# A list scheduler's table: sampled values asked for earlier, first keys and queries later, raw weights assumed later, first token load behind a weight block

## The chip, the cores and the metric

The kernel runs on one NeuronCore of a Trainium2 chip. The metric is the device time of one execution in microseconds (us); lower is better. TensorE (PE) multiplies matrices, VectorE (DVE) and ScalarE (ACT) work elementwise, GpSimd (POOL) does small copies and subtractions, and SyncE (SP) issues every DMA of this kernel. PSUM is the memory that PE writes to, SBUF the one that all engines share. A semaphore is how one engine, or a DMA that has landed, lets another go on.

## The reference

Block-sparse attention in float32, over 4 batches, 8 heads, 768 positions and 64 dimensions, feeds a two-layer MLP over the 3072 tokens.

```python
block, n_blocks, window = 32, 24, 1
mask = np.abs(blk_i - blk_j) <= window
mask = mask | (blk_i == 0) | (blk_j == 0) | (blk_i == n_blocks - 1) | (blk_j == n_blocks - 1)
for qb in range(n_blocks):
    for kb in sampled_blocks[qb]:                 # three sampled key blocks for each block of queries
        mask[qb * block:(qb + 1) * block, kb * block:(kb + 1) * block] = True
scores = np.where(mask, scale * (q @ k.T), -1e9)
attn = softmax(scores); attn_out = attn @ v
...
h = x @ w_in                                      # 512 -> 2048
r = np.maximum(h, 0.0)
out = (s * (r * r) + b) @ w_out                   # 2048 -> 512
```

## The kernel before, in words

**Attention.** The work is cut into 52 slots (`T["ORD"]`). Slots 0 to 25 are batches 0 and 1, slots 26 to 51 batches 2 and 3. A slot is either dense (kind "d": the rows that see all 768 keys, loads `qr..d` and `v` of 384 KB), sparse (kind "s": tile row t = 0 to 4, 352 key columns) or the last tile row (kind "h"). The first four slots are dense. For slot i, PE runs s(i), the scores (L694 and L708 with plain keys `kt`, L720 with sampled keys `kg`), t(i), the transposes of the exponentials (L771), a(i), the product with the values (L805 and L816 with plain values, L830 with the sampled values `vg`), and xT(i), a transpose of the result (L842). PE's line is fixed by hand as t(i), xT(i-1), s(i+2), a(i). DVE takes the row maxima (L735) and scales the result (L836), ACT does the exponentials (L747), both copy transposed tiles `pt` out of PSUM (L777, L775), ACT copies the result (L847, tile `xst`), and SP writes it to DRAM as `xd` (L859, the spill).

**Sampled values.** `gather_v` reads the sampled value blocks of one tile row for two batches in 12 DMAs of 128 KB (L637), each at an address that SP has loaded from `vidx` (L630), which DVE computes from the sampled block numbers (`sbi`). There are two `vg` buffers; `vg0` names tile row 0 of the first batches' pair.

**Weights.** `w_in` and `w_out` come as float64. `decode_f64` turns each of 32 blocks (`i0` to `i15`, `o0` to `o15`, order `T["WL"]`) into a high and a low float32 half in nine steps: L75, L77, L78, L83 (the high half), L84, L85 (the low half) on DVE, L79, L81, L82 on ACT. A raw block of 512 KB (L57, `raw_i5`, `raw_o14`) sits in one of three buffers `kraw`, which are shared with the two token loads `xraw0` (L348, 384 KB each: the `xd` of batch 0's first half read back). ACT and DVE split `xraw0` into the halves `x0` (L361 on ACT, L363 on DVE).

**MLP.** A sub is one group of 384 tokens by one of 16 blocks of 128 hidden columns f. mlp1 multiplies tokens by `w_in` (L389 to L391, three products for the halves), ACT takes the relu (L394), DVE the square (L398), ACT adds b and rounds (L402, L403), POOL subtracts for the low half (L407), and mlp2 multiplies by `w_out` (L424 to L426). The first 30 subs are ordered by the planner: subs 0 to 3 are f = 0 and 1 of groups 0 and 1, then f counts up with groups 0 and 1 in turn, so that subs 26 and 27 are f = 13, subs 28 and 29 f = 14. The rest is a fixed loop.

**The planner.** Class `Plan` is given every operation with its engine, an assumed cost, a priority number (in units: a slot has 2 or 4 units, N is their count) and what it depends on. In each step it takes, on the engine that can start first, the operation with the lowest number among those that can start then. What comes out is the program order of each engine, which the chip then follows in order. SP's DMAs use eight semaphores in rotation, so an issue waits until the DMA eight before it has landed. The numbers touched here:

```python
"LATE": 3000.0     # ns added to the assumed landing of a raw weight block
"GV": [7.0, ...]   # units ahead of first use at which the vg gathers of tile row t fall due
"KL": [46.0, ...]  # the same for the keys kt of batch b
"QL": 18.0         # the same for queries; slot 0 has 50 instead
```

The function that holds all of this, as the diff touches it:

Of the kernel before, what the change touches and what calls it, by code (L numbers as in the profile page):

```python
# [24 lines left out]
F32_MOST = float(0x7F7FF000)  # L25
T = {
# [6 lines left out]
}  # L33
# [65 lines left out]
class Plan:  # L99
# [15 lines left out]
    def op(self, eng, cost, prio, fn, deps=(), alloc=(), use=(), order=(), nbytes=0, cols=0, late=0.0):  # L115


        o = Plan.Op()
        o.cost, o.prio, o.fn, o.nbytes, o.cols, o.late = cost if isinstance(cost, dict) else {eng: cost}, prio, fn, nbytes, cols, late
        o.pick = isinstance(cost, dict)  # L120
        o.deps, o.order, o.alloc = [d for d in deps if d], [d for d in order if d], alloc
        o.end, o.seq = None, len(self.ops)
        for k in (*alloc, *use):
            self.users.setdefault(k, []).append(o)
        self.ops.append(o)
        return o
# [76 lines left out]
def kernel(  # L203
# [131 lines left out]
    def decode(which, f):  # L335
        tail = (lambda: scratch("kraw", 2 * NW, f"raw_{which}{f}").bitcast(I32), *parts())
        if which == "i":
            src, view = w_in[:, f * P:(f + 1) * P].rearrange("(c p) n -> p c n", p=P), win
        else:
            src, view = w_out[f * P:(f + 1) * P, :], wout  # L340
        return decode_f64(nc, NW, src, b_top, b_most, *tail, lambda: view(f, 0), lambda: view(f, 1))
# [101 lines left out]
    with ExitStack() as es:  # L443
# [35 lines left out]
        def load_q(key, par):  # L479
            kind, b, t = key  # L480
            if par == 0:
                qraw[key] = qp.tile([P, NPAIR, P], F32, tag="qr", name=f"qr{b}_{t}{kind}")
            rows = slice(par * D, (par + 1) * D)
            nc.sync.dma_start(out=qraw[key][rows], in_=q_dup[b, t, rows, par::2, :] if kind == "s" else q_edge[b, int(kind == "d"), rows, par::2, :])
# [380 lines left out]
        op = plan.op  # L865
# [39 lines left out]
        for b in range(B):  # L905
            need = min(first[("k", b, p)] for p in range(NPAIR))
            for p in range(NPAIR):
                prev_k = kld[(b, p)] = op("s", 450, need - T["KL"][b] + T["KS"] * p, lambda b=b, p=p: load_k(b, p),
                                          alloc=[] if p else [(f"kt{b}", b)], use=[(f"kt{b}", b)] if p else [], order=[prev_k], nbytes=557e3)
# [7 lines left out]
        for need, b, t in sorted((n, *k[1:]) for k, n in first.items() if k and k[0] == "g"):  # L917
# [3 lines left out]
            for m in range(nq * NSL):  # L921
                pk = op("g", 230 if m else 1100, need - T["GK"] + m * 0.5, lambda gk=gk, m=m: gk(m), [o_si, *(kld[(b, p)] for p in range(NPAIR))],
                        alloc=[("kg", key)] if m == 0 else [], use=[(f"kt{b}", b)] + ([("kg", key)] if m else []), order=[pk])
# [6 lines left out]
            for m in range(nq * NSL + (nq if t == NSP else 0)):  # L930
                pv = op("s", 510 if m else 1300, need - T["GV"][t] + m * 0.5, lambda gv=gv, m=m: gv(m), [o_si],
                        alloc=[("vg", key)] if m == 0 else [], use=[("vg", key)] if m else [], order=[pv], nbytes=131e3)
# [4 lines left out]
        pq = pvl = o_m = o_e = o_rc = o_ev = None  # L937
        spills, tensor, lqs = {}, {}, {}
# [3 lines left out]
        for i, (kind, b, t, x) in enumerate(slots):  # L942
            u, full, cost, col = unit_of[i], kind == "s", costs[kind], cols[kind]
            nu, ng, nk = (2, 2, 2) if kind == "d" else (4, 1, 2)
            qk = slots[i][:3]
            if qk not in lqs:
                for par in range(2):
                    pq = lqs[qk] = op("s", 450, u - (T["QL"] if i else 50) + 0.1 * par, lambda qk=qk, par=par: load_q(qk, par), alloc=[] if par else [("qr", qk)],
                                      use=[("qr", qk)] if par else [], order=[pq], nbytes=131e3)
            lq = lqs[qk]  # L950
            lv = {}
# [7 lines left out]
            for k in range(nk):  # L959
# [3 lines left out]
                       alloc=[("B", ("s", *y)) for y in keys], use=[("qr", qk), (f"kt{b}", b)])  # L963
# [10 lines left out]
            for j in range(nu):  # L974
                n, ms_ = u + j, []
                for g in range(ng):
                    o_m = op("v", {"s": 600, "d": 680, "h": 500}[kind], n + T["MP"], lambda n=n, g=g: maximum(n, g),
                             [*s_of[(n, g)], *([] if kind == "d" else [o_ss]), *ms_],
                             alloc=[("P", (n, g))] + ([("nm", n)] if g == 0 else []), use=[("B", ("s", n, g))] + ([("nm", n)] if g else []),
                             order=[o_m])  # L980
                    ms_.append(o_m)
                for g in range(ng):
                    top = g == 0 and j == 0
                    o_e = op("a", {"s": 780, "d": 800, "h": 700}[kind], n + T["EP"], lambda n=n, g=g: exp(n, g), ms_,
                             alloc=[("dn", i)] if top else [], use=[("P", (n, g)), ("nm", n)] + ([] if top else [("dn", i)]), order=[o_e])
# [9 lines left out]
            for j in range(nu):  # L995
                pr = j if kind == "d" else 0
                o = op("p", cost[3], u, lambda i=i, j=j: av_static(i, j), cols=col[3], deps=[*evs[j], lv[pr]],
                       alloc=[] if j else [("o", i)], use=[("v", (i, pr)), *(("pt", (u + j, g)) for g in range(ng))] + ([("o", i)] if j else []))
# [30 lines left out]
        xl, xs_ops = {}, {}  # L1029
        sp_of = [[spills[i] for i, sl in enumerate(slots) if sl[1] == b] for b in range(B)]  # L1030
        for g in range(2):
            for c2 in range(2):
# [3 lines left out]
                else:  # L1036
# [3 lines left out]
                        alloc=[] if c2 else [key], use=[key] if c2 else [], order=[xl[(1, 0)]] if c2 else [pv], nbytes=393e3)  # L1040
# [7 lines left out]
        for k, (which, f) in enumerate((w[0], int(w[1:])) for w in T["WL"].split()):  # L1048
            load, st = decode(which, f)
            raw, wp = ("kraw", (which, f)), ("wp", (which, f))  # L1050
            pw = op("s", 450, N + T["WP"] - 4 + T["WS"] * k, load, [prev_k], alloc=[raw], nbytes=524e3, late=T["LATE"])
            mine = {}
            for m, (eng, fn, needs) in enumerate(st):
                alloc, deps, order = [], [pw, *(mine[x] for x in needs)], []
                if m == 0:
                    alloc = [wp]
                if m == 1:
                    order = [mine[0]]
                if which == "o" and m == 6:
                    if f % 2:  # L1060
                        order = [wdone[("o", f - 1, 6)]]
                    elif f == 2:
                        deps += [xs_ops[(1, c, 1)] for c in range(NCC)]
                    elif f == 4:
                        alloc, order = [("vg", "wos1")], [xl[(1, 0)]]
                    elif f == 6:
                        order = [wdone[("o", 5, 6)]]
                    elif f == 8:
                        order = attention
                    elif f > 8:  # L1070
                        order = [wdone[("o", f - 1, 6)]]
                    else:
                        order = [xl[(1, 0)]]
                if which == "i" and m == 6:
                    if f % 4 == 0:
                        alloc = [(f"kt{f // 4}", ("win", f // 4))]
                    else:
                        order = [wdone[("i", f - 1, 6)]]
                mine[m] = wdone[(which, f, m)] = op(eng, cost[m], N + T["WP"] + T["WS"] * k + 0.3 * m, fn, deps, alloc=alloc, order=order,
                                                    use=[raw] * (m in (0, 1, 2, 3, 6)) + [wp] * (m > 0) + [("vg", f"wos{f // 4}")] * (which == "o" and m == 6 and f < 8 and f != 4))  # L1080
        NPL = T["NPL"]
        pm, pm2 = o_m, None
        hd, m2 = {}, {}
        for k in range(NPL):
            g, f = subs[k]
# [6 lines left out]
            if k > 0:  # L1092
                g, f = subs[k - 1]
# [22 lines left out]
    for i in range(NPL, NSUB + LAG):  # L1116
        s = SUB0 + i
# [92 lines left out]
```

## Time and profile before

| | |
|---|---|
| median of 3 runs | 828.12 us (822.63 to 832.83) |
| profiled execution, its own time | 827.27 us |
| span, first to last instruction | 825.5 us |
| granted clock, mean | 0.993 |
| PE busy | 803.8 us, 97% |
| DVE busy | 408.0 us, 49% |
| ACT busy | 472.9 us, 57% |

The span is 1.77 us shorter than the execution's own time, so terms read in the span are added to 827.27. Attention takes the span up to 282.3 us, where the first mlp1 starts; the MLP takes the rest. PE's own idle time in the whole span is 21.7 us, and a half-clock stretch of PE shows in the granted clock, not in idle time.

### The profile page before, as it was taken

To read this page: it belongs to the slowest core of one execution; us is meant where nothing else is said; L and a number is where in the kernel's file an instruction comes from. 1 tells how busy PE (TensorE), PEld (TensorE's weight loads), DVE (VectorE), ACT (ScalarE), POOL (GpSimd) and SP (SyncE) were. 2 spreads that over 40 slices of the span, in tenths; PEclk is the share of its full clock that TensorE was granted. 3 is DMA by queue.
4 is the path that set the end of the run, shared out by engine and by line. 5 is a ranking of instruction groups with operands and counts; after the bars stand their busy time and mean duration, and the time that the engine had idled before them with its cause. 6 is when DMAs were issued, how large, how long until landed. Compare 5 with 4: busy or idle time off the path is not lost.

```text
span 825.5 us, 21605 instructions
## 1 busy us (share of the span) xinstructions
PE 803.8 (97%) x8512; PEld 699.8 (85%) x8512; DVE 408.0 (49%) x1061; ACT 472.9 (57%) x1107; POOL 206.8 (25%) x436
## 2 busy tenths in 40 slices
PE   7889999999999999999999999999999999999998
PEld 5677877888876889999989999999999999999996
DVE  4666778888987899999631221212212112122111
ACT  3666768878886788778554434434434444444433
POOL 1722133222300032222222222222222222222221
PEclk9999999999999999999999999999999999999999
DMA  8997897877777423433130010002002002001001
GB/s 253 271 234 279 225 254 199 246 234 226 213 198 225 142 102 102 129 107 123 39 115 1 1 66 11 1 1 77 0 1 77 1 1 77 0 1 39 1 1 38
DMA packets 79061, 89.03 MB, mean 108 GB/s; under 512 B 10736, under 2 KB 57968, under 8 KB 78960
## 3 DMA queue, kind: packets, MB, share of 16 engines
q1 hardware_dynamic: 78960, 87.66, 36.3%
q8 instruction: 67, 1.10, 0.6%
q14 instruction: 34, 0.28, 0.1%
HBM read 75.05 MB, written 12.58 MB: 106 GB/s over the span
## 4 chain that ended last, share of the span: by engine, by line
PE 88%; DMA 4%; SPq 3%; issue 2%; DVE 1%; ACT 1%; POOL 0%; DVEq 0%; POOLq 0%; ACTq 0%
PE o L425 11%; PE o L426 11%; PE o L424 11%; PE h L391 10%; PE h L389 10%; PE h L390 10%; PE t L771 8%; PE xs L816 5%; PE s L694 4%; PE xs L830 3%; PE s L720 2%; DMA kt<-in_k_seq_dram 2%; PE s L708 1%; DMA vg<-in_v_dram 1%; SPq L637 1%
## 5 line engine op out<-in xcount | busy, mean ns | idle before, releaser
L407 POOL TENSOR_TENSOR hid<-hid,hid 128x384 fp32r<-128x384 f32 x128 | 135.2, 1057 | 465.9 <-ACT hid L403 456.4
L398 DVE SCALAR_TENSOR_TENSOR hid<-hid,sb_s 128x384 f32<-128x384 f32 x128 | 83.3, 652 | 306.0 <-ACT hid L394 305.8
L389 PE MATMUL h<-x,win 128*128 128x384 f32 x512 | 172.7, 337 | 0.6 <-ACT hid L394 0.6
L391 PE MATMUL h<-x,win 128*128 128x384 f32 x512 | 172.7, 337 | 0.0
L390 PE MATMUL h<-x,win 128*128 128x384 f32 x512 | 172.1, 336 | 0.2 <-DVE x L363 0.2
L394 ACT ACTIVATE hid<-h 128x384 f32<-128x384 f32 x128 | 62.7, 490 | 153.7 <-PE h L391 152.1
L747 ACT ACTIVATE ptile<-ptile,nm 128x352 f32<-128x352 f32 (+2 forms) x208 | 120.8, 583 | 32.5 <-DVE nm L735 31.6
L402 ACT ACTIVATE hid<-hid,sb_b 128x384 f32<-128x384 f32 x128 | 78.8, 616 | 72.9 <-DVE hid L398 72.9
L389 PEld LDWEIGHTS h<-x,win 128*128 128x128 f32 x512 | 96.2, 188 | 6.5 <-ACT hid L394 0.9
L390 PEld LDWEIGHTS h<-x,win 128*128 128x128 f32 x512 | 96.1, 188 | 5.8 <-DVE x L363 0.6
L391 PEld LDWEIGHTS h<-x,win 128*128 128x128 f32 x512 | 96.0, 188 | 0.0
L654 POOL COPY kg<-kt 128x128 f32 x264 | 63.6, 293 | 128.0 <-PE s L720 123.9
L735 DVE CUSTOM_DVE_ANT_0 ptile<-s,ms 128x352 f32<-128x352 f32 x160 | 74.4, 521 | 27.3 <-PE s L720 27.0
L771 PE MATMUL t<-ident,ptile 128*128 128x128 f32 x608 | 79.7, 280 | 1.7 <-DVE nm L735 0.9
L426 PE MATMUL o<-wout,hid 128*128 128x512 f32 x192 | 75.9, 395 | 0.0
L426 PE MATMUL o<-woutr,hid 128*128 128x512 f32 x192 | 75.9, 395 | 0.0
L425 PE MATMUL o<-wout,hid 128*128 128x512 f32 x192 | 75.8, 395 | 0.0
L425 PE MATMUL o<-woutr,hid 128*128 128x512 f32 x192 | 75.8, 395 | 0.0
L424 PE MATMUL o<-wout,hid 128*128 128x512 f32 x192 | 74.7, 389 | 0.0
L424 PE MATMUL o<-woutr,hid 128*128 128x512 f32 x192 | 74.6, 389 | 0.0
L771 PEld LDWEIGHTS t<-ident,ptile 128*128 128x128 f32 x608 | 66.5, 142 | 7.9 <-ACT ptile L747 2.2
L403 ACT CAST hid<-hid 128x384 fp32r<-128x384 f32 x128 | 65.8, 514 | 4.4 <-PE o L425 0.4
(131 smaller groups left out, 1080.8 us busy)
## 6 DMA issues: line engine op xcount, KB each, us to landing
vg<-in_v_dram SPq DMA_DIRECT2D x136, 128.0 KB, 3.7
v<-in_v_sta_dram SPq DMA_DIRECT2D x40, 256.0 KB, 4.3
kt<-in_k_seq_dram SPq DMA_DIRECT2D x16, 544.0 KB, 7.3
raw_i<-in_w_in_dram SPq DMA_DIRECT2D x16, 512.0 KB, 4.0
raw_o<-in_w_out_dram SPq DMA_DIRECT2D x16, 512.0 KB, 3.2
v<-in_v_dram SPq DMA_DIRECT2D x16, 384.0 KB, 6.1
xd<-xst SPq DMA_DIRECT2D x44, 128.0 KB, 3.9
xraw<-xd SPq DMA_DIRECT2D x14, 384.0 KB, 4.1
```

The lines of the kernel that those rows point to most:

```text
L389: nc.tensor.matmul(ph, wh, xh, start=(c == 0), stop=False)
L390: nc.tensor.matmul(ph, wh, xl, start=False, stop=False)
L391: nc.tensor.matmul(ph, wl, xh, start=False, stop=(c == NCC - 1))
L398: nc.vector.scalar_tensor_tensor(out=t, in0=t, scalar=sb_s, in1=t, op0=ALU.mult, op1=ALU.mult)
L402: nc.scalar.activation(t, t, AF.Identity, bias=sb_b)
L407: nc.gpsimd.tensor_tensor(out=htile(5 + i % 3), in0=t, in1=gh.bitcast(F32), op=ALU.subtract)
L424: nc.tensor.matmul(acc, gh[:, tsl], wout(f, 0), start=(f == 0), stop=False)
L425: nc.tensor.matmul(acc, gh[:, tsl], wout(f, 1), start=False, stop=False)
L426: nc.tensor.matmul(acc, gl[:, tsl], wout(f, 0), start=False, stop=(f == NFC - 1))
L735: nc.vector.tensor_tensor_reduce(out=pt[:, :w], in0=sps.pop((n, g))[:, :w], in1=msk, scale=-scale, scalar=FMAX if g == 0 else nm[:, 0:1], ...
L747: nc.scalar.activation(pt[:, :w], pt[:, :w], AF.Exp, bias=nms[n][:, last:last + 1], scale=-1.0, accum_out=dns[i][:, g, j:j + 1])
L771: nc.tensor.transpose(tp[:, c, :], src[:, c * P:(c + 1) * P], ident)
```

## The change: four numbers of the planner's table and one order

The planner assumes that a raw weight block lands 5000 ns after its transfer instead of 3000 (`LATE`). The gathers of `vg0` fall due 9 units ahead of their use instead of 7. The keys of batch 0 fall due 26 units ahead instead of 46, and slot 0's queries 18 units ahead, as all others, instead of 50. The two `xraw0` loads may not be planned before the load of raw block `i7`.

```diff
-    ... "NPL": 30, "LATE": 3000.0, ...
-    "GK": 9.0, "GV": [7.0, 15.0, 15.0, 15.0, 15.0, 15.0], "KL": [46.0, 18.0, 26.0, 26.0], "QL": 18.0, ...
+    ... "NPL": 30, "LATE": 5000.0, ...
+    "GK": 9.0, "GV": [9.0, 15.0, 15.0, 15.0, 15.0, 15.0], "KL": [26.0, 18.0, 26.0, 26.0], "QL": 18.0, ...
...
-                    pq = lqs[qk] = op("s", 450, u - (T["QL"] if i else 50) + 0.1 * par, ...
+                    pq = lqs[qk] = op("s", 450, u - T["QL"] + 0.1 * par, ...
...
             pw = op("s", 450, N + T["WP"] - 4 + T["WS"] * k, load, [prev_k], alloc=[raw], nbytes=524e3, late=T["LATE"])
             mine = {}
+            if which == "i" and f == 7:
+                for c2 in range(2):
+                    xl[(0, c2)].order.append(pw)
```

The order of instructions moves on SP, DVE and ACT. PE's order changes in 14 rows only (one transpose near the end of attention, and two mlp1 pieces that come ahead of the first mlp2), POOL's not at all.

**SP near 26 us.** Names: `qr` queries, `v` plain values, `sb_s` and `sb_b` the scalars s and b, `kt2` keys of batch 2. Before:

```order
L474 DMA kt1_179<-in_k_seq_dram 128x1088 x2
L484 DMA qr1_0s_289<-in_q_dup_dram 64x4x128 x2
L484 DMA qr0_1s_304<-in_q_dup_dram 64x4x128 x2
L492 DMA v2_0_361<-in_v_dram 128x6x128
L492 DMA v2_1_386<-in_v_dram 128x6x128
L1022 DMA sb_s_62<-in_s_dram 128x1
L1023 DMA sb_b_63<-in_b_dram 128x1
L859 DMA xd_68<-xst0_416 128x2x64
L474 DMA kt2_428<-in_k_seq_dram 128x1088
L630 TENSOR_LOAD vidx_145
L637 ISA
L637 DMA vg0_0_466<-in_v_dram 32x2x512
```

After:

```order
L474 DMA kt1_183<-in_k_seq_dram 128x1088 x2
L484 DMA qr1_0s_369<-in_q_dup_dram 64x4x128 x2
L630 TENSOR_LOAD vidx_145
L637 ISA
L637 DMA vg0_0_381<-in_v_dram 32x2x512
L492 DMA v2_0_427<-in_v_dram 128x6x128
L492 DMA v2_1_457<-in_v_dram 128x6x128
```

The first `vg0` gather now stands behind slot 4's queries, ahead of `v2`; the two scalars and the first part of `kt2` come after the last gather.

**ACT, between the exponentials of units 167 and 171** (slots 43 and 44; `pt165` and `pt167` are what a(43) on PE reads). Before:

```order
L747 ACTIVATE ptile7_85,dn43_6080<-ptile7_85,nm167_6091 128x352
L79 ACTIVATE raw_i5_5514<-raw_i5_5514 128x512
L747 ACTIVATE ptile0_78,dn44_6194<-ptile0_78,nm168_6161 128x352
L747 ACTIVATE ptile1_79,dn44_6194<-ptile1_79,nm169_6190 128x352
L747 ACTIVATE ptile2_80,dn44_6194<-ptile2_80,nm170_6196 128x352
L777 COPY pt165_0_6228<-t165_0_6202 128x384
L847 COPY xst42_6236<-xs42_6151 128x256
L777 COPY pt167_0_6241<-t167_0_6213 128x384
```

After:

```order
L747 ACTIVATE ptile7_85,dn43_6085<-ptile7_85,nm167_6102 128x352
L361 CAST x0_0_6167<-xraw0_0_6012 128x384 x2
L747 ACTIVATE ptile0_78,dn44_6196<-ptile0_78,nm168_6169 128x352
L747 ACTIVATE ptile1_79,dn44_6196<-ptile1_79,nm169_6192 128x352
L747 ACTIVATE ptile2_80,dn44_6196<-ptile2_80,nm170_6202 128x352
L777 COPY pt165_0_6230<-t165_0_6204 128x384
L847 COPY xst42_6238<-xs42_6153 128x256
L777 COPY pt167_0_6241<-t167_0_6215 128x384
```

The token split L361 stands where L79 of `raw_i5` stood. On SP, its load `xraw0` stands right behind the last `vg` gather of tile row 4 of the second batches' pair; before it was issued at 176.15 us, a place that `raw_i5` has now, while `raw_i6` has the place of the second `xraw0` load (197.78 us) and `raw_i7` that of `raw_i5`.

**DVE, the end of the decode** (`raw_o13`, `raw_i15`, `raw_o14`, `raw_o15` are the last blocks, `wkhp` and `wklp` their working halves, `win` and `woutr` the decoded weights; an L398 on `hid1` squares an odd sub, on `hid0` an even one). Before, from the square of sub 27, through that of 28, to that of 29:

```order
L398 SCALAR_TENSOR_TENSOR hid1_7088<-hid1_7088,sb_s_62 128x384
...
L83 TENSOR_TENSOR woutr_7562<-wkhp1_2705,raw_o14_7945 128x512
L84 TENSOR_SCALAR wkhp1_2705<-woutr_7562 128x512
L85 SCALAR_TENSOR_TENSOR woutr_7562<-wklp1_2715,wkhp1_2705 128x512
L398 SCALAR_TENSOR_TENSOR hid0_7051<-hid0_7051,sb_s_62 128x384
L83 TENSOR_TENSOR woutr_7562<-wkhp1_2705,raw_o15_7973 128x512
L84 TENSOR_SCALAR wkhp1_2705<-woutr_7562 128x512
L85 SCALAR_TENSOR_TENSOR woutr_7562<-wklp1_2715,wkhp1_2705 128x512
L398 SCALAR_TENSOR_TENSOR hid1_7088<-hid1_7088,sb_s_62 128x384
```

After, from the square of sub 29 on (six more rows, the last of block `o15`, stand behind it and ahead of the square of sub 30):

```order
L398 SCALAR_TENSOR_TENSOR hid1_7080<-hid1_7080,sb_s_62 128x384
L77 TENSOR_SCALAR wklp1_2718<-raw_o14_8002 128x512
L78 SCALAR_TENSOR_TENSOR wklp1_2718<-wklp1_2718,raw_o14_8002 128x512
L83 TENSOR_TENSOR win3_7836<-wkhp0_2708,raw_i15_7979 128x512
L84 TENSOR_SCALAR wkhp0_2708<-win3_7836 128x512
L85 SCALAR_TENSOR_TENSOR win3_7836<-wklp0_2717,wkhp0_2708 128x512
L83 TENSOR_TENSOR woutr_7596<-wkhp1_2709,raw_o14_8002 128x512
L84 TENSOR_SCALAR wkhp1_2709<-woutr_7596 128x512
L85 SCALAR_TENSOR_TENSOR woutr_7596<-wklp1_2718,wkhp1_2709 128x512
```

Block `o14` was complete ahead of the square of sub 28, and is now complete eight rows behind that of sub 29; `o15`, complete ahead of the square of sub 29 before, follows behind it too.

## Rows read from the trace of the kernel before

**Rows 1.** The page, part 4: the chain that ended last, by engine.

```profile
PE 88%; DMA 4%; SPq 3%; issue 2%; DVE 1%; ACT 1%; POOL 0%; DVEq 0%; POOLq 0%; ACTq 0%
```

**Rows 2.** Windows; columns: stretch, length, busy us by engine, granted clock, DMA share, GB/s.

```profile
20.00:40.00 20.00, 17.36 (x259) 12.15 (x255) 13.92 (x52) 12.52 (x39) 16.09 (x67) 0.91 1.07 271
40.00:60.00 20.00, 17.82 (x391) 14.59 (x389) 11.30 (x42) 11.45 (x36) 5.87 (x25) 0.91 0.94 238
240.00:260.00 20.00, 18.07 (x371) 14.51 (x368) 14.08 (x49) 13.77 (x41) 0.00 (x0) 0.91 0.84 258
380.00:400.00 20.00, 20.00 (x102) 18.12 (x101) 18.60 (x32) 15.87 (x29) 5.81 (x5) 1.00 0.30 97
```

**Rows 3.** Waits of PE, whole span; columns: total us, times, longest us.

```profile
PE xs L830 <- DMA vg<-in_v_dram: 3.4, 3, 2.2
```

**Rows 4.** Timeline of PE, front; columns: start, us, what, [idle before, releaser].

```profile
28.48 2.72 PE L708 MATMUL s<-kt,qr_5d 64*64 64x384 f32 x14 [1.44 <-DMA kt<-in_k_seq_dram]
...
46.83 0.31 PE L830 MATMUL xs<-vg,pt 96*32 96x64 f32 x6
49.32 1.03 PE L830 MATMUL xs<-vg,pt 96*32 96x64 f32 x26 [2.18 <-DMA vg<-in_v_dram]
```

**Rows 5.** Timeline of PE, 243 to 254 us.

```profile
243.22 1.15 PE L816 MATMUL xs<-v,pt 128*64 128x64 f32 x32
244.30 0.65 PE L830 MATMUL xs<-vg,pt 96*32 96x64 f32 x32
...
246.56 1.13 PE L694 MATMUL s<-kt,qr_4s 64*128 64x256 f32 x8
...
251.86 0.52 PE L771 MATMUL t<-ident,ptile 128*128 128x128 f32 x3 [0.88 <-DVE nm L735]
253.44 0.44 PE L842 MATMUL xs<-ident,xss 128*128 128x128 f32 x2 [1.06 <-DVE xss L836]
253.81 2.00 PE L694 MATMUL s<-kt,qr_4s 64*128 64x256 f32 x8
```

**Rows 6.** Timeline of DVE at 250.5 us.

```profile
250.51 0.43 DVE L75 TENSOR_SCALAR wkhp<-raw_i 128x512 int32<-128x512 int32 x1 [3.47 <-DMA raw_i<-in_w_in_dram]
```

**Rows 7.** Timeline of ACT, 238 to 242.5 us.

```profile
238.09 0.68 ACT L79 ACTIVATE raw_i<-raw_i 128x512 f32<-128x512 f32 x1
...
241.77 0.37 ACT L847 COPY xst<-xs 128x256 f32<-128x256 f32 x1 [0.34 <-PE xs L842]
242.04 0.48 ACT L777 COPY pt<-t 128x384 f32<-128x384 f32 x1
```

**Rows 8.** Timeline of SP's DMA issues, 239 us.

```profile
239.17 0.32 SPq L637 DMA_DIRECT2D vg<-in_v_dram  x1
```

**Rows 9.** Issues of L348, the token loads, in its line's view: landing times.

```profile
DMA to landing us min/median/max: 3.5/4.2/7.1
```

**Rows 10.** Token splits of L361 on ACT; columns: ns min/median/max, first and last start.

```profile
L361 ACT CAST x<-xraw x28: 501/506/513, 223.5 to 732.1; 128x384 fp32r<-128x384 f32 x28
```

**Rows 11.** Timeline of PE, first mlp1, third quarter.

```profile
285.40 0.34 PE L389 MATMUL h<-x,win 128*128 128x384 f32 x1
```

**Rows 12.** Timeline of DVE, end of the decode.

```profile
395.36 1.39 DVE L78 SCALAR_TENSOR_TENSOR wklp<-wklp,raw_o 128x512 f32<-128x512 int32 x1
...
397.54 0.41 DVE L77 TENSOR_SCALAR wklp<-raw_o 128x512 int32<-128x512 int32 x1
...
398.60 0.68 DVE L83 TENSOR_TENSOR woutr<-wkhp,raw_o 128x512 fp32r<-128x512 f32 x1
...
401.62 0.69 DVE L83 TENSOR_TENSOR woutr<-wkhp,raw_o 128x512 fp32r<-128x512 f32 x1
...
403.41 1.38 DVE L398 SCALAR_TENSOR_TENSOR hid<-hid,sb_s 128x384 f32<-128x384 f32 x1
```

**Rows 13.** Lines of DVE, 300 to 403.5 us; columns: count, busy us, mean ns, idle before.

```profile
L85 DVE SCALAR_TENSOR_TENSOR woutr<-wklp,wkhp 128x512 fp32r<-128x512 f32 x8 | 7.0, 881 | 0.3
```

**Rows 14.** Timeline of PE, the first product of mlp2 of sub 28.

```profile
406.58 0.39 PE L424 MATMUL o<-woutr,hid 128*128 128x512 f32 x1
```

More of the change, by code (lines that the diff above doesn't have):

```diff
@@ L947 @@
                 for par in range(2):
-                    pq = lqs[qk] = op("s", 450, u - (T["QL"] if i else 50) + 0.1 * par, lambda qk=qk, par=par: load_q(qk, par), alloc=[] if par else [("qr", qk)],
+                    pq = lqs[qk] = op("s", 450, u - T["QL"] + 0.1 * par, lambda qk=qk, par=par: load_q(qk, par), alloc=[] if par else [("qr", qk)],
                                       use=[("qr", qk)] if par else [], order=[pq], nbytes=131e3)
```

4 rows, old and new, of the table T are left out of this document.

## Prediction

> **What bounds the kernel now.** I read the chain of waits first. It is PE's for 88% [rows 1], so a change counts by what it does to PE's idle time and to PE's clock, and idle time of DVE, ACT or SP counts only where PE waits for it. The windows say where PE is not full [rows 2]: 17.4 of 20 us at 20 to 40, 17.8 at 40 to 60, 18.1 at 240 to 260, and the full 20.0 in the MLP at 380 to 400. The first three windows also have a granted clock of 0.91, and the MLP 1.00. The missing 0.09 of 20 us is 1.8 us of PE work, as about 3.6 us at the lower of the two clock levels (1.2 GHz) would make it. Each such stretch follows an idle stretch of PE.
>
> The timelines name these waits. At the front PE waits 1.44 us for the last keys of batch 1 (start at 28.48) and 2.18 us for a gather of `vg0` (start at 49.32) [rows 4], the longest of three waits for gathers, 3.4 us in all [rows 3]. Behind that of 49.32 the 26 matmuls of L830 take 1.03 us; at full clock 32 of them take 0.65 [rows 4, 5], so 26 take 0.53. At 251.86 and 253.44 PE waits 0.88 and 1.06 us for DVE [rows 5], and DVE had stood 3.47 us on the landing of a raw weight block, `raw_i6` [rows 6]. Eight matmuls of L694 then take 2.00 us instead of 1.13 [rows 5]. I price a lower-clock stretch at 1.6 us: most of the 1.8, since PE is not busy in all of it.
>
> **The change part by part**, as a sum against the profiled execution's 827.27 us.
>
> *Front.* All 12 `vg0` gathers move on SP ahead of the scalars, of the first part of `kt2` and of most of `v2` and `v3`. Before, the last four stood behind all of these. They should now land before a(4), which wants them at 46.83. The stall and its clock stretch go: −2.2 − 1.6 = −3.8. What is late next there is `v4`, whose load still stands ahead of a(4). The wait for the last keys at 28.48 stays, as the queue ahead of them carries the same bytes in another order. The table load `sbi` goes ahead of the keys, so the first maxima can start sooner; bounds are nothing and the whole 1.44 us of that key wait [rows 4]. I take −0.5, nearer to nothing, because PE is held by keys and not by maxima.
>
> *Raw weights and the token load.* `raw_i6` and `raw_i7` take earlier places on SP (that of `raw_i6` is the one of 197.78), so DVE no longer waits for `raw_i6`: −0.88 − 1.06 − 1.6 = −3.5. But the first `xraw0` load now stands right behind the last gather, which was issued at 239.17 [rows 8]; with its 0.32 us and a gap the token load goes out at about 239.55. ACT's split L361 of these tokens stands where L79 of `raw_i5` stood, and ACT came there at 238.09 [rows 7]. The 14 token loads took 3.5 us at the least, 4.2 in the median and 7.1 at the most [rows 9]; at the median the tokens land at 243.75. ACT therefore stands about 5.6 us, and queued behind are three exponentials, a copy of `pt165`, one of `xst42` and one of `pt167`. Before, these ran from 238.77 (the end of L79) to 242.52 (the end of `pt167`'s copy) [rows 7], 3.75 us, of which ACT waited 0.34 for PE, so 3.4. After two splits of 0.506 us [rows 10], `pt167` is ready at 243.75 + 1.0 + 3.4 = 248.15. PE's a(43) starts at 243.22 and takes 1.15 us in four quarters [rows 5]; the last, which reads `pt167`, would start at 244.08. The stall is 4.1 us (3.4 with the fastest landing, 7.0 with the slowest). I take the median, since in this place no 512 KB block runs beside the load. A lower-clock stretch behind it, +1.6: shorter stalls had one [rows 4, 5]. Together +5.7.
>
> Two rules of the Trainium skill bear here. That what is queued behind a waiting instruction waits too is shown for DVE, where PE waited for maxima queued behind the L75 on `raw_i6` [rows 5, 6]; no row shows it of ACT. "TensorE: Matmul & The Clock Gate", section "Architectural detail: the array is 16× 32×32, not 1× 128×128", states that ScalarE is strictly first in, first out; without that rule the sum would be 5.7 us lower. And for the landing, where the rows say 4.2 us, "DMA: Bandwidth & Descriptors", section "Anatomy of one DMA — SWDGE (gpsimd) path", gives about 2.0 us plus the bytes at 436 GB/s for another way of issuing, as an estimate 2.9 us for 393 KB; by it the stall would be 2.8 us and the sum 1.3 lower, within the forecast's bounds. The rows decide, as all 14 loads took longer.
>
> *Start of the MLP.* The second `xraw0` load moves behind the spill of slot 49, into the buffer that `raw_i6` leaves, two slots before the end of attention at 282.3; I put its issue at 281 and its landing, 4.2 us on [rows 9], at 285.2. The split on ACT (0.5) and on DVE (by the step of L83, 0.7 [rows 12]) follow, to 286.4, and the third quarter of the first mlp1 stood at 285.40 [rows 11]. What makes attention end later moves both. By these numbers it is +1.0, and nothing if the load goes out a microsecond sooner; bounds 0 and 1.5 (the second split as well), I take +0.5.
>
> *End of the decode.* Since `raw_o0` is loaded at the end of attention and no longer within it, DVE's decode steps stand later among the squares. The critical one is the low half of `o14`, which mlp2 of sub 28 reads at 406.58 [rows 14]. Before, it was written ahead of the square of sub 28, which ended ahead of the L83 at 401.62 [rows 12], some 5 us to spare. Now it stands eight rows behind the square of sub 29, which started at 403.41, as early as mlp1 and relu allow [rows 12]. Eight rows: twice L83, L84, L85, 1.79 us each time by the step from 401.62 to 403.41, and L77 and L78, 1.06 us by the step from 397.54 to 398.60 [rows 12]; together 4.64. One row is likely to meet POOL's L407 and take 1.39 instead of 0.69, as L78 at 395.36 did [rows 12], +0.7. With 0.6 for the square `o14` is ready at 403.41 + 0.6 + 4.64 + 0.7 = 409.35, a stall of 2.8 us. Without the slow row it is 2.1; with every row at the stretch's mean, by L85's 0.881 against 0.69 [rows 12, 13], and a slow square of 1.38, it is 4.1. A lower-clock stretch behind it is not certain in a stage at 1.00 with long matmuls on both sides; I take +1.0 of 1.6. Blocks `i15` and `o15` follow by about 413 us, and mlp2 of sub 30 comes later than that.
>
> **Sum:** 827.27 − 3.8 − 0.5 − 3.5 + 5.7 + 0.5 + 2.8 + 1.0 = 829.5. The median of the three runs is 0.85 above the profiled execution, so the forecast, 830.3, is **830 us**: two stalls go, two of like size come.
>
> **The rivals.** *The new waits don't happen (faster):* the tokens land before ACT comes to L361, because SP, with fewer loads ahead, reaches the gathers sooner, and DVE keeps up. For it: SP issues late only because of what it waits for. Against: in the order no load between 200 and 239 us goes away, and the gathers' due time is the same. 827.27 − 3.8 − 0.5 − 3.5 + 0.5 + 0.85 = 821 us. With only one of the two waits absent it is 825 to 826.
>
> *The decode comes later still (slower):* POOL's L407 runs once per sub, and a DVE row beside it takes 1.39 us [rows 12]. If not one but all eight rows run at the doubled length, they take 9.3 us, and with a slow square of 1.38 `o14` is ready at 414.1, a stall of 7.5 with a sure clock stretch: 830 + 4.7 + 0.6 = 835 us. It decides from 406.58 − 403.41 = 3.2 us on: each microsecond past that is one of PE's. Against it: the means of [rows 13] are 1.3 times the short form, not twice it.
>
> *The change doesn't do at the front what it says:* PE finds at a(4), or ahead of it, another transfer that is late (`v4`, or `kt1`), since the same bytes must come through the same queue by then. The front's 3.8 us stay: 834 us. For it: the windows' queue is full there, a DMA share of 0.94 to 1.07 [rows 2]. Against: the first part of `kt2` is out of the way.
>
> **How the numbers follow.** The forecast with its bounds (825 to 832) has 0.45, the fast case 0.20, the slow one 0.15, the unchanged front 0.15, and 0.05 is left. The range goes from 821 to 837: it cuts off half of the fast case and the slow case's tail (a token load of 7.1 us as well, 838). Runs of this kernel lie 10 us apart at the most, 2% is 16.6 us, about what a measurement can tell from no change; only several of these cases together reach 811.6 or 844.7, so 0.02 faster, 0.95 same, 0.03 slower.
>
> **What would show it.** In the changed profile: no wait of L830 for `vg` near 47 us, and a clock of 1.00 at 40 to 60; no wait of DVE for `raw_i`; an L361 on ACT that waits about 5 us for `xraw` near 239 to 244, a wait of PE's L816 for a copy L777 there, and a low clock behind it; one wait of L424 for DVE near mlp2 of sub 28, 2 to 4 us. The prediction is wrong if SP issues the token load well before 239, if ACT is behind at that place so that the wait is hidden, or if the front shows a new wait of PE.

## The result and the profile after

The changed kernel takes 833.14 us in the median of 22 runs (828.51 to 836.82), the kernel before, run beside it, 826.67 (822.63 to 834.06). The ratio is 1.0063, with a 95% interval of 1.0042 to 1.0085: slower by about 5 us (6.5 by the two medians), less than 2%. The forecast was 830, range 821 to 837. The profiled execution took 832.62 us (span 830.9), 5.35 more than that of before.

The page's chain of waits, by engine (as [rows 1] of before): PE's share fell from 88% to 85%, DVE's rose from 1% to 4%, ACT's to 2%.

```profile
PE 85%; DMA 5%; DVE 4%; SPq 3%; ACT 2%; issue 2%; ACTq 0%; DVEq 0%
```

The windows (columns as in [rows 2]; the last one was undisturbed before, at 1.00):

```profile
20.00:40.00 20.00, 17.94 (x285) 12.29 (x283) 11.66 (x41) 11.98 (x38) 8.62 (x36) 0.88 0.98 259
40.00:60.00 20.00, 20.00 (x498) 16.56 (x479) 14.71 (x55) 14.45 (x44) 5.93 (x25) 1.00 0.84 209
...
240.00:260.00 20.00, 15.63 (x347) 13.20 (x344) 12.14 (x41) 14.89 (x46) 0.00 (x0) 0.83 0.53 160
...
400.00:420.00 20.00, 17.60 (x78) 14.90 (x77) 15.02 (x25) 11.19 (x22) 3.50 (x4) 0.91 0.20 66
```

One window is better and two are worse. At 40 to 60 PE is now full and at full clock. At 240 to 260 it is busy for 15.6 us where it was 18.1, at a clock of 0.83 instead of 0.91, and at 400 to 420 for 17.6 us at 0.91. PE's list of waits over the whole span (columns as in [rows 3]) has the causes:

```profile
PE xs L816 <- ACT xst L847: 4.4, 1, 4.4
PE xs L830 <- DMA vg<-in_v_dram: 2.5, 3, 1.8
PE t L771 <- ACT ptile L747: 1.9, 1, 1.9
PE s L708 <- DMA kt<-in_k_seq_dram: 1.8, 2, 1.2
PE o L424 <- DVE woutr L83: 1.7, 1, 1.7
...
PE xs L816 <- DMA v<-in_v_sta_dram: 0.8, 1, 0.8
...
PE o L425 <- DVE woutr L85: 0.7, 1, 0.7
```

**The token split.** SP, ACT, PE and DVE around 240 us, in their timelines, in this order:

```profile
236.84 0.32 SPq L637 DMA_DIRECT2D vg<-in_v_dram  x1
237.26 0.56 SPq L348 DMA_DIRECT2D xraw<-xd  x1
```

```profile
235.02 0.60 ACT L747 ACTIVATE ptile<-ptile,nm 128x352 f32<-128x352 f32 x1
235.51 0.20 ACT L747 ACTIVATION_READ_ACCUMULATOR ptile<-ptile,nm 128x1 f32 x1
241.84 0.93 ACT L361 CAST x<-xraw 128x384 fp32r<-128x384 f32 x2 [6.13 <-DMA xraw<-xd]
242.67 0.58 ACT L747 ACTIVATE ptile<-ptile,nm 128x352 f32<-128x352 f32 x1
...
244.75 0.36 ACT L847 COPY xst<-xs 128x256 f32<-128x256 f32 x1
245.02 0.48 ACT L777 COPY pt<-t 128x384 f32<-128x384 f32 x1
```

```profile
237.50 1.53 PE L771 MATMUL t<-ident,ptile 128*128 128x128 f32 x12
...
240.24 0.56 PE L720 MATMUL s<-kg,qr_4s 64*32 64x96 f32 x32
245.17 1.98 PE L816 MATMUL xs<-v,pt 128*64 128x64 f32 x32 [4.37 <-ACT xst L847]
247.08 1.08 PE L830 MATMUL xs<-vg,pt 96*32 96x64 f32 x32
248.09 2.39 PE L771 MATMUL t<-ident,ptile 128*128 128x128 f32 x12
```

```profile
237.19 0.52 DVE L735 CUSTOM_DVE_ANT_0 ptile<-s,ms 128x352 f32<-128x352 f32 x1
```

The token load goes out right behind the last gather at 237.26, and ACT, which stands 6.13 us on it, starts the split 4.6 us after that. The last of the next four maxima was started by 237.19, so the exponentials had their inputs, and the first still came at 242.67: ACT did not pass a waiting instruction. PE waits 4.37 us, up to the copy L847 of `xst42`, and the three stages behind take 1.98, 1.08 and 2.39 us, 2.1 more than the 1.15, 0.65 and 1.53 that a slot takes at full clock ([rows 5] for the first two; L771 at 237.50 for the third). Measured from the start of the same PE instruction in both traces, the changed kernel is 2.4 us ahead just before a(43) and 4.1 behind one slot later: 6.5. The wait of before for `raw_i6` [rows 5, 6] is gone, and by 258 us the changed kernel is only 0.2 behind.

**The end of the decode.** DVE, POOL, then PE (as [rows 12, 14] of before):

```profile
404.63 0.61 DVE L398 SCALAR_TENSOR_TENSOR hid<-hid,sb_s 128x384 f32<-128x384 f32 x1
...
407.40 1.38 DVE L85 SCALAR_TENSOR_TENSOR win<-wklp,wkhp 128x512 fp32r<-128x512 f32 x1
...
409.88 0.69 DVE L85 SCALAR_TENSOR_TENSOR woutr<-wklp,wkhp 128x512 fp32r<-128x512 f32 x1
```

```profile
407.17 1.06 POOL L407 TENSOR_TENSOR hid<-hid,hid 128x384 fp32r<-128x384 f32 x1 [3.34 <-ACT hid L403]
```

```profile
409.44 0.49 PE L424 MATMUL o<-woutr,hid 128*128 128x512 f32 x1 [1.71 <-DVE woutr L83]
...
410.62 0.79 PE L425 MATMUL o<-woutr,hid 128*128 128x512 f32 x1 [0.69 <-DVE woutr L85]
```

Behind the square of sub 29 come eight decode rows, one of them at the doubled length (1.38, while POOL's L407 runs), and mlp2 of sub 28 waits twice, 2.4 us. With the lower clock behind it the kernel falls from 1.0 us behind to 5.4.

**The front.** The first sampled product finds its data (PE's timeline, against the 46.83 and 49.32 of [rows 4]), but a later one does not:

```profile
45.96 0.65 PE L830 MATMUL xs<-vg,pt 96*32 96x64 f32 x32
...
138.91 0.61 PE L830 MATMUL xs<-vg,pt 96*32 96x64 f32 x26 [1.85 <-DMA vg<-in_v_dram]
```

By the same matching of PE instructions (times of before) the changed kernel is 4.8 us ahead at 52.7 us and 2.4 ahead at 243. The lead does not shrink evenly. It first grows to 6.9 by 115 us, chiefly because before has a wait of 1.97 us there (at 114.91) that the profile gives no releaser for. Then it falls: by the longer wait at 138.91 (1.85 where before's was 0.66, at 142.68) and by waits of 0.6, 0.6, 0.8 and 0.4 us without a releaser. Such waits move about from profile to profile.

### The profile page after: what moved, and what is told of

It is laid out like the page before. It is cut to its first block, busy times and chain, and to the rows that moved or that the text cites. A ratio compares the mean times of both kernels' runs of the same rounds, so it can differ in the third digit from the quotient of the medians.

```text
span 830.9 us, 21602 instructions
## 1 busy us (share of the span) xinstructions
PE 806.1 (97%) x8512; PEld 701.4 (84%) x8512; DVE 406.8 (49%) x1061; ACT 473.0 (57%) x1107; POOL 207.2 (25%) x436
## 4 chain that ended last, share of the span: by engine, by line
PE 85%; DMA 5%; DVE 4%; SPq 3%; ACT 2%; issue 2%; ACTq 0%; DVEq 0%
PE o L425 10%; PE o L426 10%; PE o L424 10%; PE h L391 10%; PE h L390 10%; PE h L389 10%; PE t L771 7%; PE xs L816 5%; PE s L694 4%; PE xs L830 3%; PE s L720 2%; DMA kt<-in_k_seq_dram 2%; PE xs L805 1%; SPq L637 1%; PE s L708 1%
## 5 line engine op out<-in xcount | busy, mean ns | idle before, releaser
L407 POOL TENSOR_TENSOR hid<-hid,hid 128x384 fp32r<-128x384 f32 x128 | 135.0, 1055 | 474.5 <-ACT hid L403 471.3
L398 DVE SCALAR_TENSOR_TENSOR hid<-hid,sb_s 128x384 f32<-128x384 f32 x128 | 84.1, 657 | 307.7 <-ACT hid L394 307.6
L771 PE MATMUL t<-ident,ptile 128*128 128x128 f32 x608 | 80.1, 281 | 3.2 <-ACT ptile L747 1.9
L771 PEld LDWEIGHTS t<-ident,ptile 128*128 128x128 f32 x608 | 66.6, 142 | 9.4 <-ACT ptile L747 3.4
```

The costliest lines, as they stand in the source:

```text
L398: nc.vector.scalar_tensor_tensor(out=t, in0=t, scalar=sb_s, in1=t, op0=ALU.mult, op1=ALU.mult)
L407: nc.gpsimd.tensor_tensor(out=htile(5 + i % 3), in0=t, in1=gh.bitcast(F32), op=ALU.subtract)
L771: nc.tensor.transpose(tp[:, c, :], src[:, c * P:(c + 1) * P], ident)
```

## The experiments

All are timed against the kernel before on the same chip; a ratio stands with its 95% interval.

**e1, the three front numbers alone** (tested again as e11).

```diff
-    "GV": [7.0, ...], "KL": [46.0, ...]      u - (T["QL"] if i else 50)
+    "GV": [9.0, ...], "KL": [26.0, ...]      u - T["QL"]
```

> The three front numbers alone (sampled values, first keys, first queries); weights and token load as before. Theory: the stall of 2.2 us at the first sampled values and its lower-clock stretch go, PE is 4 to 5 us ahead at 53 us, and about 2 of these are given back at the next sampled values that come late (tile row 3) and at small waits: 2 to 3 us faster than before in all, ratio 0.996 to 0.998. Rival: PE just meets later transfers sooner and gives all of it back: no change, 1.000. Second rival: nothing is given back: 4.5 us faster, 0.9945.

821.15 us against 827.5, ratio 0.9927 (0.9892 to 0.9961); again, in e11, 823.54 against 827.98, 0.9951 (0.9919 to 0.9984). The two together say 4 to 6 us faster: the rival that gives nothing back is nearer than the theory. In e1's profile PE is 3.6 us ahead at 52.7 us (times of before), 4.0 at 243 and 6.5 from 258 on. The last 2.5 are gained where before waits for `raw_i6`: e1 has only the second of the two waits there, 1.06 us, and the clock stays at full speed behind it, though no number of e1 is meant for that place. So the measured gain need not be the front's alone. Between 52.7 and 240 us e1 gains 0.4 us, and e11 0.6. So what the changed kernel's profile lost there is not a lasting price of the front.

> The three front numbers alone once more, beside the two kernels with h last and on their chip: 0.992 to 0.996 by both theories, as before; it tells whether the other two differ from it.

**e2, only `LATE` 5000.**

> Only the assumed landing of raw weights, 5000 for 3000 ns. Theory: DVE's order of the last decode steps comes from this number alone, so the wait of mlp2 of sub 28 (2.4 us) and the lower clock behind it (2.0) show here by themselves, with attention unchanged: 4.4 us slower, ratio 1.005. Rival (the prediction's wording): the decode is late because the token load pushes the first block of w_out behind the end of attention; then this kernel is as fast as before, 1.000, and the next one carries the wait.

831.99 against 827.5, ratio 1.0042 (1.0007 to 1.0077), the theory. SP's order is that of before from end to end, so the loads of `raw_o0` and of the tokens stand where they stood; the other engines' orders are those of before up to the end of attention. PE's timeline still has the wait, within a hundredth of the changed kernel's; with the lower clock behind it e2's trace loses 4.5 us against before between 404 and 420 us (times of before):

```profile
411.90 0.50 PE L424 MATMUL o<-woutr,hid 128*128 128x512 f32 x1 [1.72 <-DVE woutr L83]
...
413.08 0.50 PE L425 MATMUL o<-woutr,hid 128*128 128x512 f32 x1 [0.69 <-DVE woutr L85]
```

**e3, only the token loads' order behind `i7`.**

> Only the token load's order behind raw block i7. Theory: ACT waits about 6 us at the token split, PE 4.4 us and a lower-clock stretch of 2.1; the wait for raw block i6 and its clock stretch go (3.5); the start of the MLP costs 0.5: 3.5 us slower, ratio 1.004, and no wait of mlp2 of sub 28. Rival: with the wait of mlp2 as well, 8 us slower, 1.010.

833.68 against 827.5, ratio 1.0075 (1.0042 to 1.0108): 6 us slower, above the 3.5 of the theory, which lies at the interval's edge, and with no wait of mlp2 for the decode, against the rival. ACT and PE in their timelines:

```profile
248.40 0.92 ACT L361 CAST x<-xraw 128x384 fp32r<-128x384 f32 x2 [6.58 <-DMA xraw<-xd]
```

```profile
251.73 1.98 PE L816 MATMUL xs<-v,pt 128*64 128x64 f32 x32 [4.82 <-ACT xst L847]
```

From a(43) to the next slot this profile loses 7.0 us against before, gets 3.9 back at `raw_i6`'s place and loses 0.3 at the start of the MLP: 3.4 in all, the theory's. The rest of its distance (3.6 us by 232 us) comes from waits ahead of that, above all for sampled values (2.07 us for before's 0.66, 1.59 for 0.56), which differ between executions of the other kernels too. Whether the median holds something beyond the theory stays open.

**e4, the front and the order, `LATE` 3000, and the planner told that token loads land late**, so that it places the split L361 behind the copy of the next slot.

```diff
-  ... lambda c2=c2: xload(0, c2), sp_of[0], alloc=[key], nbytes=393e3)
+  ... lambda c2=c2: xload(0, c2), sp_of[0], alloc=[key], nbytes=393e3, late=5000.0)
```

> The front numbers and the order, raw weights assumed as before (3000), and the planner told that a token load lands 5000 ns later, so that it places the token split on ACT some 16 instructions later. Theory: the 6.5 us of the split's wait and the 4.4 us of the decode are both gone, the front and raw block i6 keep their gains: 827 - 2.5 - 3.5 + 0.5, about 821.5 us, ratio 0.993 to 0.995. Rival: the load lands later still or ACT's order costs elsewhere, and the wait stays at half: ratio 0.998.

823.43 against 827.5, ratio 0.9935 (0.9901 to 0.9969), the theory. That is no faster than the front numbers alone (0.9927 and 0.9951): in e4's profile the start of the MLP gives 2.1 us back, with waits for the token split (0.8) and for decoded weights (1.2). ACT's timeline shows the split near 246 us with no wait ahead of it:

```profile
246.37 0.92 ACT L361 CAST x<-xraw 128x384 fp32r<-128x384 f32 x2
```

**e8, the whole change with `LATE` back at 3000.**

> The whole change but for the assumed landing of raw weights, which is 3000 again. Theory: the decode's wait near 409 us is gone and all else is as in the changed kernel: 4.4 us less than it, 828.5 us, ratio to before 1.001 to 1.003, with the wait at the token split near 241 us still there. Rival: the token load behind i7 makes the decode late too: ratio 1.006, as the whole change.

827.05 against 825.85, ratio 1.0015 (0.9989 to 1.0041), the theory. PE still waits at the split, 5.42 us, and nowhere for the decode. e8 and e4 differ only in what the planner is told of the token loads; their ratios differ by 0.8%, some 6.6 us, against the 6.5 of the changed kernel's trace. In e8's own trace the split costs 8.0, from 7.1 ahead to 0.9 behind.

```profile
241.59 1.98 PE L816 MATMUL xs<-v,pt 128*64 128x64 f32 x32 [5.42 <-ACT xst L847]
```

**e5, only the due time of the sampled values** (`GV` 9 for 7).

> Only the due time of the first sampled values, 9 units for 7. Theory: it moves nothing ahead of the scalars and of kt2 on SP (in the order the first gather stands behind kt2 as before), so the 2.2 us wait near 49 us stays: ratio 1.000. Rival (as the change reads): this number is what takes the wait away, with the lower clock 3.8 us: 0.9955.

826.09 against 825.85, ratio 0.9995 (0.9964 to 1.0026): nothing. The gathers stay behind the scalars and `kt2` (only the last of the 12 moves, ahead of `v6`), and PE waits for them. The wait is 1.03 us here, where it was 2.18 before; e2 and e3, with the front order of before, have 1.58 and 1.52:

```profile
49.78 0.61 PE L830 MATMUL xs<-vg,pt 96*32 96x64 f32 x26 [1.03 <-DMA vg<-in_v_dram]
```

**e6, only the 73 KB load of the sampled block numbers first.**

```diff
-        sb_load = op("s", 450, -30, load_sampled, ...
+        sb_load = op("s", 450, -60, load_sampled, ...
```

> Only the priority of the 73 KB load of the sampled block numbers, ahead of everything, keys, queries and sampled values due as before. Theory: that load's place is what the later keys and queries really change, since DVE then has the addresses early and the planner puts the gathers ahead of v2; so this equals the three front numbers together: ratio 0.991 to 0.996. Rival: the later keys and queries gain by themselves at the start: this gives half of it, 0.997.

822.9 against 825.85, ratio 0.9968 (0.9943 to 0.9994), by its middle where the rival put it, with the upper part of the theory's range inside the interval. The gathers move ahead of `v2` as in the change, and the wait is gone:

```profile
48.24 0.65 PE L830 MATMUL xs<-vg,pt 96*32 96x64 f32 x32
```

So it is the place of `sbi`, which the later keys and queries bring about, that moves the gathers. Its gain is at the weak end of e1's and e11's. Its profile has waits of 3.3 us for plain values of the first slots where e1's has 0.2, so the later keys and queries may bring the rest themselves; the intervals overlap, and this stays open.

**e7, the front, `LATE` 3000, and the token loads behind `i5`.**

```diff
-            if which == "i" and f == 7:
+            if which == "i" and f == 5:
```

> The front numbers, raw weights assumed as before, and the token loads behind raw block i5 instead of i7: the tokens are loaded before 220 us, only raw i5 comes earlier, and DVE takes up raw i6 at the end of attention, long after it has landed. Theory: no wait at the token split and none for raw i6: 827 - 6 - 3.5 = 817.5 us, ratio 0.988 to 0.990. Rival: raw i6 decoded at the end of attention delays the MLP's start by as much: ratio 0.992, as the front alone.

820.29 against 825.85, ratio 0.9929 (0.9896 to 0.9961), where the rival put it, though the interval reaches 0.990, the edge of the theory. Its profile has neither the split's wait nor that for `raw_i6` (from 240 to 258 us of before it gains 3.9 us), but its front is only 2.3 us ahead at 52.7 us, where e1's is 3.6. Whether it beats the front numbers alone the runs don't tell.

**e9 and e10, the front and the last tile row (slots of kind h) moved behind tile row 4**, in the first half of the slots (e9) or in both (e10).

```diff
-    "... a30 a31 b30 b31 aH bH a40 a41 b40 b41",
+    "... a30 a31 b30 b31 a40 a41 b40 b41 aH bH",
```

> The front numbers, and in the first half of the slots the last tile row (kind h) moved behind tile row 4. There are two buffers for sampled values, so the values of row 4 can only be fetched when row 3 is done; before, only the two short h slots lie between, and PE waited there 0.7 to 2.9 us in all but one of the profiles so far, at times with a lower clock behind it. Theory: that wait goes: 1 to 2 us less than the front numbers alone, ratio 0.988 to 0.992, and no wait of L830 for vg near 140 us. Rival: h then has the short time, or the token loads come later by the h slots: 0.993 or more.

> As the one before, with h behind row 4 in the second half too, where it stood between rows 2 and 3. Theory: its smaller wait (about 0.5 us near 230) goes as well: ratio 0.987 to 0.991. Rival: no difference to the one before.

820.49 and 819.25 against 827.98, ratios 0.993 (0.9903 to 0.9958) and 0.9913 (0.9879 to 0.9947), the front alone beside them 0.9951. e9 lies where its rival begins, and e10 differs from e9 by less than either interval. The wait near 140 us is gone from both profiles, but e6, e8 and e11 have none there either, and e1 only 0.15 us without a releaser; "all but one of the profiles" in the expectation was not right. That the kernels are faster than the front alone is likely for e10 by its middle, but the intervals overlap. e10 is the fastest version measured, by the ratios some 7 us below the kernel before and 12 below the changed one.

## Why the prediction was right

The time lay 3 us above the forecast, inside the range and just above the forecast's own bounds (825 to 832), and five of the six terms were there. As a step from the kernel before, the forecast was only 2 us (830 against 828.1) and the measured one 5 to 6.5; that the time itself came out so near is in part luck, since the kernel before ran 1.5 us faster beside the changed one than in the three runs that the forecast started from. In the order of the sum, with what the changed kernel's profile shows by matching PE instructions of both traces:

| term | predicted, us | measured, us |
|---|---|---|
| front, up to 53 us | −4.3 | −4.8 |
| 53 to 240 us | 0 | +2.4 |
| `raw_i6` | −3.5 | −3.9 |
| token split | +5.7 | +6.5 |
| start of the MLP | +0.5 | +0.8 |
| end of the decode | +3.8 | +4.4 |
| sum | +2.2 | +5.4 |

*Front.* The wait and its lower-clock stretch went, and `v4` was not late in their place, so the rival of an unchanged front fell. The reason was only half told: the gathers do not move by their own due time (e5 changes nothing) but because `sbi` is loaded first (e6).

*53 to 240 us.* Here a term is missing. I had taken this stretch as unchanged, since its order hardly changes. But PE meets the sampled values of tile row 4 at a place where they are just late, and how late differs by execution: in the profiles with h ahead of row 4 the wait was 0.66 before, 1.85 in the changed kernel, 2.75 in e2, 2.07 in e3, 2.94 in e4, 1.67 in e5, 0.93 in e7, and none in e6, e8 and e11. With the front numbers in, the lead over before changes between 52.7 and 240 us by −2.3 us in the changed kernel, −2.1 in e4, +0.1 in e7, +0.4 in e1, +0.6 in e11 and +2.9 in e8. And e2, whose order up to the end of attention is that of before on every engine, is 5.1 us behind it at 240 us. So a difference of 2.4 between two single profiles need not come from the change. The sum of the separate ratios agrees: e1 or e11 (−0.73%, −0.49%), e2 (+0.42%) and e3 (+0.75%) add to +0.44% or +0.68%, and the whole change is +0.63%. But each has an interval of 0.3% to either side, so this sum can't tell 2.4 us.

*`raw_i6`.* The wait went, and the size was right against this profile of before. But 1.6 of it is the lower clock, and that is not sure to follow: e2, e6 and e11 wait there for the same two rows and stay at full clock, and their profiles gain 1.6 to 1.7 us on before's at this place without the change of order.

*Token split.* The mechanism was as predicted but for the last link. ACT waited 6.1 us for a forecast of 5.6: ACT came 2.4 us sooner than reckoned (235.71) and SP 2.3 us sooner (237.26), so the difference lies in the landing, 4.6 us for 4.2. PE's wait was 4.4 for 4.1. It did not stand at the last quarter of a(43) for the copy L777 of `pt167`, as predicted, but at the first for the copy L847 of `xst42`; the two copies stand side by side on ACT (244.75 and 245.02), so the size hardly differs. The lower clock cost 2.1 and not 1.6: the price was taken as less than the 1.8 of a window because PE would not be busy throughout, and here it was, from 245.2 to 250.3 at a granted clock of 0.54. The Trainium skill's rule that ScalarE is strictly first in, first out ("TensorE: Matmul & The Clock Gate", section "Architectural detail: the array is 16× 32×32, not 1× 128×128") agrees with the trace: exponentials with inputs ready by 238 ran at 242.67. The price of a DMA in the Trainium skill ("DMA: Bandwidth & Descriptors", section "Anatomy of one DMA — SWDGE (gpsimd) path"), as an estimate 2.9 us and given for another way of issuing, does not: the split waited until 4.6 us after the issue.

*End of the decode.* `o14` was ready at 410.57, against 409.35 plus the 1.0 us by which the kernel was then late, with the one doubled row that the sum had. The wait was 2.4 for 2.8, the lower clock 2.0 for 1.0. But the sentence that named its cause was wrong: "since `raw_o0` is loaded at the end of attention" is not why the steps stand later. e2 has `raw_o0` at its old place and the wait in full; e3 and e8 have it at the end of attention and no wait. From 404 to 420 us e2 loses 4.5 us against before, and e3, e4 and e8 less than 0.1. The number `LATE` does it: the planner believes the block to be there 2 us later, and, as I read its rule, puts squares, which are ready, first. I read the order of the whole change, where the two parts cannot be told apart.

The slow rival, all eight rows doubled, fell with one doubled row of eight. In the fast one SP did issue sooner, at 237.26 for 239.55, which was named as a sign of being wrong, but ACT too came sooner.

## What to carry to other kernels

A planner's number acts on the order, not on the chip: build each number's order by itself before pricing it, since the one whose name fits may move next to nothing (`GV`) and another, through what it lets become ready, may move everything (`KL` and `QL` through a 73 KB load). Where engines run in program order, an assumption that errs early costs a standing engine and everything queued behind it (the token split), and one that errs late costs the place in the line (`LATE`); correcting the assumption for the one load that was late took the wait away (e4), though the kernel was then no faster than without the new order. And a change that shifts a phase by some microseconds meets every place where data is just in time again, so a sum from one profile needs an error of a few microseconds for those (e2 and before, 5 us apart at 240 us with one and the same order).

## What the runs showed that I had not expected

A wait of PE is not always followed by the lower clock, and its length alone does not tell: after 1.85 us of waiting at 138.91 the changed kernel's windows at 120 to 160 us stay at 1.00, after 2.75 in e2 the same stretch is at 0.91, and before, waits of 0.88 and 1.06 us, with 1.6 us between their ends, brought the clock to the lower level. In e5, 1.03 us of waiting near 49 us left the following L771 at its 1.53 us, while 1.58 us there in e2 made it 1.94. At `raw_i6`'s place even one and the same pair of waits ends both ways. In before and in e5 the window at 240 to 260 us has 0.91; in e2, e6 and e11 it has 1.00. PE in e2, against the 2.00 us of L694 in [rows 5]:

```profile
256.82 0.52 PE L771 MATMUL t<-ident,ptile 128*128 128x128 f32 x3 [0.78 <-DVE nm L735]
258.40 0.44 PE L842 MATMUL xs<-ident,xss 128*128 128x128 f32 x2 [1.06 <-DVE xss L836]
258.77 1.13 PE L694 MATMUL s<-kt,qr_4s 64*128 64x256 f32 x8
```

So a price for the lower clock behind a wait, read from one profile, holds for that profile; how often it comes the runs don't tell.
